# A new hand-written order for an attention and gated-MLP kernel, with idle products as words of the order

## The chip, the cores and the metric

One core of a Trainium2 chip runs the kernel. A core has five engines that run at the same time, each taking its own instructions in order: TensorE (PE, matrix products; its weight loads are listed as PEld), VectorE (DVE), ScalarE (ACT), GpSimd (POOL), and SyncE (SP), which here only starts DMA transfers. SBUF is the on-chip memory of 128 partitions; PSUM has eight banks per partition into which PE writes. The metric is the device time of one execution in microseconds, as the median of several runs.

## The reference

Attention with normalised q and k, and then a gated MLP whose second half is mixed along the sequence. Cut to what matters:

```python
# q, k, v: (8, 12, 448, 64)
q_n, k_n = rmsnorm(q, g_q), rmsnorm(k, g_k)
scores = (1 / sqrt(64)) * q_n @ k_n.transpose(0, 1, 3, 2)
attn = softmax(scores)
x = (attn @ v).transpose(0, 2, 1, 3).reshape(8, 448, 768)

h = maximum(x @ w_in, 0)                  # 768 -> 1024
u, v2 = h[..., :512], h[..., 512:]
v_n = (v2 - mean(v2)) / sqrt(var(v2) + 1e-6)
v_s = einsum('ts,bsd->btd', w_spatial, v_n) + b_spatial[None, :, None]
out = (u * v_s) @ w_out                   # 512 -> 768
```

rmsnorm divides a row of 64 by its root mean square and multiplies by a vector of gains.

## The kernel before

The work is cut into 24 groups, three for each of the eight batch entries; a group holds four heads. In a group, q and k are loaded (word L, 448 KB each), squared (Q, on ACT, DVE or POOL), summed over each row of 64 (R, DVE), turned into 1/rms by a logarithm and an exponential (I and J, ACT), and multiplied by it (N, DVE or POOL). Then they are transposed, either on PE (P, followed by the eviction K on DVE) or by a DMA transpose (T; Z then applies the gains to k). A group has seven score words: S.G.u on PE makes two PSUM banks of scores from 8 products of 64 rows by 32 columns, and E.G.u takes the exponential of both banks on ACT. Three kinds of passes on PE sum over the exponentials of one such unit: s with ones (the softmax's denominators), a and b with the two halves of v, which F converts to bf16. D and d on ACT invert the denominators through a logarithm and an exponential, X on DVE multiplies and leaves the MLP's input. Groups 0 and 1 pass one group at a time; from group 2 on, two groups share a pass.

The MLP of a batch entry b is made of V (the half v2, 2 products a word), c (its relu), B (statistics), M and m (1/std), A (normalising); U (the half u, 2 products a word) and u (its relu); H (the mixing along the sequence, 4 products), G (the gate, DVE), O (the output product, 4 products), o (eviction) and t (store). W.b holds the last 64 rows of the products V of entry b and O of entry b - 1.

Small letters l, q, r, i, j, n, p, k are the same steps for group 0, cut into two halves (r = 0 and 1) so that work can begin on the first half of the load. z.n and h.n are idle products: n products of the identity into a PSUM bank (448 and 64 columns, lines 250 to 259), whose result nobody reads.

All of this is issued from one string, PLAN, a list of words. A word is name.arguments/slots/engine: `E.3.6/3/a` is the exponential of unit 6 of group 3 into buffer 3 on ACT (a is ACT, v DVE, g POOL, s SP). The loop at lines 719 to 722 issues word by word, so that the order of the words of one engine in the string is the order in which that engine runs them:

```python
for word in PLAN.split():
    name, sl, e = (word.split("/") + ["", ""])[:3]
    name, *args = name.split(".")
    here["op_" + name]([int(x, 36) for x in sl], e, *map(int, args))
```

Waits between engines follow from the tiles that the words read and write, and from one more rule: the elementwise passes of DVE and POOL over SBUF (Q, N, F, Z, A) each wait for the last such pass of the other engine in the string (`port`, lines 281 to 285). The numbers of buffers are fixed (`SLOTS`, line 152): 10 raw loads, 22 buffers of exponentials, 8 PSUM banks shared by all.

Lines to follow the text by: 253 idle products, 293 loads of a group, 306 half loads of group 0, 365 and 367 copies (on ACT, on another engine), 384 and 386 squares, 397 and 403 sums, 410 and 415 logarithm and exponential of I and J, 430 and 438 normalising passes, 449 and 457 transposes on PE, 468 evictions of k, 510 scores, 518 exponentials, 545 summing passes, 564 and 568 D and d, 574 X, 581 relu on ACT, 590 V, 619 W, 656 U, 670 H, 684 O.

Of the kernel before, what the change touches and what calls it, by code (L numbers as in the profile page):

```python
# [22 lines left out]
l.0.0/0/a l.1.0/1 gl.0//g l.0.1//a l.1.1 L.1.0/2 gl.1//g setup L.1.1/3 L.2.1/4 L.2.0/5 z.12/0 L.3.0/6 q.0.0/0/v  # L23
L.3.1/7 q.1.0/1/a r.0.0 L.4.0/8 r.1.0 q.0.1//a L.4.1/9 i.0//a r.0.1 j.0//a q.1.1//v n.0.0//v r.1.1 p.0.0/0 Q.1.0/2/a
n.1.0//g gA gB/1 i.1//a R.1.0 p.1.0/2 j.1//a k.0.0/0/a n.0.1//g gC Q.1.1/0/a k.1.0/0/v n.1.1//g L.0.2/0 p.0.1/0
Q.2.1/1/a R.1.1 S.0.1/12 L.5.0/1 p.1.1/3 E.0.1/0/a Q.2.0/2/g k.0.1//v I.1//a k.1.1//v J.1//a R.2.1 Q.3.0/0/a
S.0.3/01 S.0.2/23 N.1.0/0/g S.0.4/45 S.0.5/67 E.0.3/1/a R.2.0 E.0.4/2/a S.0.0/01 ws N.1.1/1/v L.1.2/2 E.0.5/3/a
P.1.0/4 wi.0.3 R.3.0 I.2//a L.6.0/3 P.1.1/5 Q.3.1/1/g E.0.0/4/a S.0.6/67 J.2//a K.1.1/1/v E.0.2/5/a s.0.0.0/0 s.0.3.0
 K.1.0/1/v N.2.1/2/g E.0.6/6/a s.0.5.0 R.3.1 S.1.6/12 s.0.1.0 s.0.4.0 E.1.6/7/a S.1.1/34 S.1.2/56 s.0.6.0 wi.1.3
s.0.2.0 N.2.0/3/v L.5.1/4 I.3//a S.1.0/12 D.0/0/a P.2.1/7 J.3//a E.1.2/8/a P.2.0/0 Q.4.0/2/g K.2.1/2/v E.1.1/9/a  # L30
S.1.3/56 K.2.0/2/v Y.3/7 E.1.3/a/a wi.1.0 N.3.0/0/v S.2.6/34 E.1.0/b/a Y.0/0 N.3.1/1/v T.3.0/3 E.2.6/c/a Y.2/1 F.0//v
d.0//a L.7.1/5 y.3//v S.2.0/23 Q.5.0/0/g R.4.0 S.1.5/45 wb/1 E.2.0/d/a Y.1/6 L.6.1/6 y.2//v L.7.0/7 E.1.5/e/a L.2.2/0
Q.6.0/1/g S.1.4/12 y.1//v b.0.2.0/3 y.0//v E.1.4/f/a P.3.1/7 R.5.0 Q.4.1/2/a a.0.4.0/0 a.0.2.0 S.2.2/12 K.3.1/3/v
Q.5.1/0/g b.0.1.0 b.0.6.0 E.2.2/g/a b.0.3.0 R.4.1 S.2.3/45 s.1.6.0/6 a.0.0.0 E.2.3/h/a a.0.1.0 a.0.6.0 R.6.0 a.0.5.0
# [718 lines left out]
```

## Time and profile before

| | |
|---|---|
| median of 3 runs | 271.17 us (270.94 to 273.24) |
| the profiled execution | 269.62 us, its span 267.8 us |
| busy PE / DVE / ACT / POOL | 252.0 / 210.1 / 219.4 / 123.9 us |
| weight loads on PE | 127.0 us |
| mean granted clock of PE | 0.977 |
| moved by DMA | 55.93 MB, 209 GB/s on average |

A profile is one execution. The span goes from the first to the last instruction; the execution's own time has 1.8 us more around it. A row of a timeline is: start, length, engine, line of the kernel, operation, output<-input, shapes, count, and in brackets the idle time of that engine ahead of it with what ended it. A row of the groups is: line, engine, operation, names, shapes, count, then busy microseconds and the mean nanoseconds of one, then the idle time ahead of such instructions and what ended most of it. In the chain of waits a row is start, length and what. A product's busy time is modelled with its pipeline, so products that follow each other closely are told by the distance of their starts.

### The profile page before, as it was taken

To read this page: it belongs to the slowest core of one execution; us is meant where nothing else is said; L and a number is where in the kernel's file an instruction comes from. 1 tells how busy PE (TensorE), PEld (TensorE's weight loads), DVE (VectorE), ACT (ScalarE), POOL (GpSimd) and SP (SyncE) were. 2 spreads that over 40 slices of the span, in tenths; PEclk is the share of its full clock that TensorE was granted. 3 is DMA by queue.
4 is the path that set the end of the run, shared out by engine and by line. 5 is a ranking of instruction groups with operands and counts; after the bars stand their busy time and mean duration, and the time that the engine had idled before them with its cause. 6 is when DMAs were issued, how large, how long until landed. Compare 5 with 4: busy or idle time off the path is not lost.

```text
span 267.8 us, 9983 instructions
## 1 busy us (share of the span) xinstructions
PE 252.0 (94%) x4282; PEld 127.0 (47%) x4282; DVE 210.1 (78%) x367; ACT 219.4 (82%) x362; POOL 123.9 (46%) x96
## 2 busy tenths in 40 slices
PE   5598998999999997999999999999999999999993
PEld 2355454345444553445544554445445645555551
DVE  5998988899999996997998777999567463636861
ACT  4889899799999997898999899999899989521512
POOL 2795975668775587644734765443450000000000
PEclk9959799999999999999999999999999999999998
DMA  7999999999999999999999989999661041120135
GB/s 258 385 319 236 299 227 222 279 200 239 229 271 197 291 243 253 242 283 277 282 221 254 267 197 231 316 236 167 228 126 68 4 179 32 62 117 2 54 154 206
DMA packets 60446, 55.93 MB, mean 209 GB/s; under 512 B 36465, under 2 KB 56242, under 8 KB 60402
## 3 DMA queue, kind: packets, MB, share of 16 engines
q1 hardware_dynamic: 58082, 51.98, 77.0%
q0 software_dynamic: 1952, 2.76, 6.1%
q8 instruction: 33, 0.54, 0.9%
q10 hardware_dynamic: 368, 0.56, 0.6%
q14 instruction: 11, 0.09, 0.1%
HBM read 38.55 MB, written 11.01 MB: 185 GB/s over the span
## 4 chain that ended last, share of the span: by engine, by line
PE 86%; ACT 5%; DVE 4%; issue 2%; DMA 2%; DVEq 0%
PE ps L545 17%; PE ps L510 14%; PE ps L656 14%; PE ps L684 12%; PE ps L590 12%; PE ps L670 9%; PE ps L619 5%; ACT et L518 4%; DMA raw<-in_q_dram 2%; PE ps L449 1%; DVE ss L397 1%; DVE nrm L430 1%; DVE kT L468 1%; DVE ss L403 0%; DVE qT L367 0%
## 5 line engine op out<-in xcount | busy, mean ns | idle before, releaser
L518 ACT ACTIVATE et<-ps 128x896 bf16<-128x896 f32 x168 | 145.5, 919 | 11.1 <-PE ps L510 10.2
L430 POOL TENSOR_TENSOR nrm<-raw,rs 128x896 bf16<-128x896 f32 x31 | 52.1, 1688 | 39.1 <-DVE nrm L430 13.7
L510 PE MATMUL ps<-qT,kT 64*32 64x448 bf16 x1344 | 60.5, 365 | 4.4 <-DVE kT L468 1.6
L386 POOL TENSOR_TENSOR sqt<-raw 128x896 f32<-128x896 f32 x29 | 48.4, 1678 | 18.2 <-DVE nrm L430 5.2
L397 DVE TENSOR_REDUCE ss<-sqt 128x14 f32<-128x896 f32 x46 | 48.7, 1074 | 0.0
L545 PE MATMUL ps<-et,vt 64*32 64x448 bf16 x1344 | 47.2, 352 | 0.4 <-issue 0.4
L656 PE MATMUL ps<-xt,w_in 128*128 128x448 bf16 x192 | 42.7, 353 | 0.0
L590 PE MATMUL ps<-w_in,xt 128*128 128x512 bf16 x144 | 37.5, 380 | 0.6 <-issue 0.6
L684 PE MATMUL ps<-w_out,gt 128*128 128x384 bf16 x192 | 36.6, 327 | 0.2 <-issue 0.2
L574 DVE TENSOR_TENSOR xt<-ps,rc 128x448 bf16<-128x448 f32 x48 | 27.9, 616 | 8.8 <-ACT rc L568 4.5
L510 PEld LDWEIGHTS <-kT 64*32 64x32 bf16 x1344 | 20.4, 91 | 29.1 <-issue 19.9
L545 PEld LDWEIGHTS <-vt 64*32 64x32 bf16 x1344 | 21.0, 93 | 14.7 <-issue 3.3
L670 PE MATMUL ps<-w_spT,vn 128*128 128x448 bf16 (+1 forms) x128 | 27.3, 353 | 0.0
L656 PEld LDWEIGHTS <-w_in 128*128 128x128 bf16 x192 | 17.6, 98 | 19.9 <-issue 4.9
L545 PE MATMUL ps<-et,ones 64*32 64x448 bf16 x672 | 25.9, 356 | 0.5 <-ACT et L518 0.5
L367 DVE COPY os<-ps 128x384 f32<-128x384 f32 (+2 forms) x36 | 19.6, 548 | 8.3 <-PE ps L619 2.9
L684 PEld LDWEIGHTS <-gt 128*128 128x128 bf16 x192 | 17.8, 98 | 16.8 <-issue 4.7
L675 DVE TENSOR_TENSOR gt<-ps,us 128x448 bf16<-128x448 f32 x32 | 19.0, 618 | 8.2 <-PE ps L670 7.3
L631 DVE BATCH_NORM_STATS2 s<-vs 128x6 f32<-128x512 bf16 (+1 forms) x32 | 21.8, 680 | 3.4 <-ACT vs L581 3.0
L365 ACT ACTIVATE os<-ps 128x384 f32<-128x384 f32 (+2 forms) x29 | 13.9, 485 | 10.2 <-PE ps L684 7.2
L590 PEld LDWEIGHTS <-xt 128*128 128x128 bf16 x144 | 12.6, 98 | 18.1 <-issue 6.7
L581 ACT ACTIVATE vs<-ps 128x512 bf16<-128x512 f32 (+1 forms) x20 | 11.8, 596 | 9.1 <-PE ps L590 8.7
(64 smaller groups left out, 260.0 us busy)
## 6 DMA issues: line engine op xcount, KB each, us to landing
raw<-in_q_dram SPq DMA_DIRECT2D x23, 448.0 KB, 6.4
raw<-in_k_dram SPq DMA_DIRECT2D x23, 448.0 KB, 6.2
out_dram<-os SPq DMA_DIRECT2D x23, 384.0 KB, 3.4
raw<-in_v_dram SPq DMA_DIRECT2D x13, 448.0 KB, 6.1
raw<-in_v_dram SPq DMA_DIRECT2D x22, 224.0 KB, 5.2
out_dram<-os SPq DMA_DIRECT2D x9, 192.0 KB, 2.7
w_in<-in_moe_w_in_dram POOLq DMA_DIRECT2D x8, 192.0 KB, 5.8
w_out<-in_moe_w_out_dram POOLq DMA_DIRECT2D x1, 768.0 KB, 12.8
```

What stands on the lines that cost most here:

```text
L386: port(eng, eng.tensor_tensor(out=t, in0=x, in1=x, op=ALU.mult))
L397: dve.tensor_reduce(out=sss[G % 3][:, i].rearrange("p r c -> p (r c)"), in_=sqt[where.pop(("sq", G, i))].rearrange("p r (c d) -> p (r c) d ...
L430: port(eng, eng.tensor_tensor(out=nrm[sl[0]].rearrange("p c r d -> p r c d"), in0=raw[where["raw", G, i]].rearrange("p r (c d) -> p r c d" ...
L510: pe.matmul(out=ps[at:at + 32, sl[n], 0:S], lhsT=kT[64 * r:64 * r + 64, c, 64 * hh + 32 * x:64 * hh + 32 * x + 32], rhs=qT[64 * r:64 * r + ...
L518: act.activation(out=ets[sl[0]].rearrange("q r (p c) -> q r p c", c=C), in_=ps[:, a:b + 1:b - a, 0:S].rearrange("q r (c p) -> q r p c", c= ...
L545: pe.matmul(out=ps[32 * l:32 * l + 32, where[kind, G][0], 0:S], lhsT=w, rhs=et_of(G, r, c)[at:at + 64], start=(n == 1), stop=(n == C), til ...
L574: dve.tensor_tensor(out=xts[b % 2][:, 2 * g + half, :], in0=ps[:, where.pop(("ab"[half], G))[0], 0:S], in1=rcs[where["rc", G]], op=ALU.mult)
L590: pe.matmul(out=ps[:, bank, :], lhsT=xts[b % 2][:, j, 128 * m:128 * m + 128], rhs=w_in[:, j % 2, j // 2, DH:], start=(n == 1 and j == 2 * ...
L631: dve.bn_stats(out=s6, in_=vss[b % SLOTS["vs"]][rows, m, :])
L656: pe.matmul(out=ps[:, bank, 0:S], lhsT=w_in[:, j % 2, j // 2, 128 * f:128 * f + 128], rhs=xts[b % 2][:, j, :], start=(n == 1 and j == 2 * ...
L670: pe.matmul(out=ps[:, sl[0], 0:S], lhsT=vns[b % SLOTS["vn"]][rows, m, 128 * f:128 * f + 128], rhs=w_spT[rows, m, :], start=(m == 0), stop= ...
L684: pe.matmul(out=ps[:, sl[0], 0:384], lhsT=gts[b % 2][:, f, 128 * m:128 * m + 128], rhs=w_out[:, f, 384 * h:384 * h + 384], start=(f == 0), ...
```

## The change

The string PLAN is replaced as a whole; the functions, `SECOND`, `SLOTS` and the sizes stay. The same words stand in both plans (1,640 and 1,644) except for the idle products: one word of 12 (z.12) before; z.11 and h.6 in its place, and z.4, z.3 and z.1 later. Each engine's order is new, and so is the choice of engine for some words: squares Q on ACT, DVE, POOL go from 12, 5, 29 to 9, 8, 29; normalising passes N on DVE, POOL from 15, 31 to 14, 32; conversions of v (F) on ACT, DVE, POOL from 1, 8, 15 to 1, 4, 19; relus of v2 (c) on ACT, DVE from 20, 12 to 17, 15; relus of u from 14, 18 to 12, 20; two of the 17 Z go from DVE to ACT. In group 0 three of the four half squares are on ACT and one on POOL (two and two on ACT and DVE before); all four half normalising passes are on POOL and all four copies k on DVE.

The lines of the plan that hold the beginning and the words which the prediction speaks of (the rest is rewritten in the same manner):

```diff
@@ -20,132 +20,132 @@
-l.0.0/0/a l.1.0/1 gl.0//g l.0.1//a l.1.1 L.1.0/2 gl.1//g setup L.1.1/3 L.2.1/4 L.2.0/5 z.12/0 L.3.0/6 q.0.0/0/v
-L.3.1/7 q.1.0/1/a r.0.0 L.4.0/8 r.1.0 q.0.1//a L.4.1/9 i.0//a r.0.1 j.0//a q.1.1//v n.0.0//v r.1.1 p.0.0/0 Q.1.0/2/a
-n.1.0//g gA gB/1 i.1//a R.1.0 p.1.0/2 j.1//a k.0.0/0/a n.0.1//g gC Q.1.1/0/a k.1.0/0/v n.1.1//g L.0.2/0 p.0.1/0
-Q.2.1/1/a R.1.1 S.0.1/12 L.5.0/1 p.1.1/3 E.0.1/0/a Q.2.0/2/g k.0.1//v I.1//a k.1.1//v J.1//a R.2.1 Q.3.0/0/a
-S.0.3/01 S.0.2/23 N.1.0/0/g S.0.4/45 S.0.5/67 E.0.3/1/a R.2.0 E.0.4/2/a S.0.0/01 ws N.1.1/1/v L.1.2/2 E.0.5/3/a
...
-L.8.0/0 E.3.6/3/a Q.7.0/0/g K.4.0/0/v b.1.6.0 s.2.0.1 s.2.2.1 X.1.0 s.2.5.1 I.6//a S.3.1/56 J.5//a s.2.3.1 X.1.1
-s.2.6.1 E.3.1/f/a S.4.1/12 F.3//g R.7.1 E.4.1/4/a s.2.1.1 S.4.4/56 b.2.6.1/07 N.5.1/1/v b.2.0.1 E.4.4/1/a
...
-J.7//a V.0.0.0/4 E.4.5/8/a N.7.1/2/v L.9.1/4 V.0.2.0 d.3//a V.0.1.0/5 L.10.1/1 X.2.1 V.0.0.1 N.6.0/3/g L.5.2/5 R.8.1
-V.0.1.1 Q.8.0/2/a V.0.0.2 S.4.6/01 X.3.1 c.0.0//a W.0/2 T.6.0/2 Z.5/1/v E.4.6/a/a X.3.0 N.6.1/1/g R.8.0 L.4.2/3
-c.0.3//a S.5.6/01 S.5.3/67 E.5.6/9/a V.0.2.2 wo L.11.0/6 P.7.1/2 c.0.2//v E.5.3/e/a Q.9.0/0/g B.0.3 S.4.0/01 S.5.2/34
...
-u.0.3//a A.0.2 S.5.0/12 I.8//a S.5.1/34 A.0.3 S.5.4/67 E.5.0/3/a A.0.0 U.0.0.2 A.0.1 U.0.1.0 E.5.4/h/a R.9.1 U.0.1.1
-P.6.1/1 E.5.1/j/a u.0.0//v F.4//g H.0.2/2 Q.10.1/1/a N.7.0/0/g H.0.0/3 L.11.1/3 G.0.2 J.8//a F.5//a K.6.1/3/v
...
+l.0.0/0/a l.1.0/1 gl.0//g l.0.1//a wb/0 l.1.1 gl.1//g setup L.1.0/2 L.1.1/3 L.2.1/4 z.11/0 h.6 L.2.0/5 q.0.0/0/a
+L.1.2/6 q.1.0/1/a r.0.0 L.3.0/7 r.1.0 L.3.1/8 q.0.1//g L.6.0/9 i.0//a j.0//a q.1.1//a r.0.1 n.0.0//g gA r.1.1 n.1.0//g
+gB/0 p.0.0/1 Q.1.0/2/a gC p.1.0/0 i.1//a R.1.0 j.1//a Q.1.1/0/a n.0.1//g z.4/2 k.0.0/0/v Q.2.1/1/a n.1.1//g L.5.0/0
+p.0.1/2 k.1.0/0/v R.1.1 ws S.0.1/01 L.4.0/1 p.1.1/3 E.0.1/0/a Q.2.0/2/g k.0.1//v S.0.2/45 I.1//a z.3/6 k.1.1//v J.1//a
...
+s.0.0.0 R.3.0 S.1.3/23 N.2.1/2/g E.0.4/6/a S.1.6/45 s.0.5.0 z.1/7 R.3.1 E.1.6/7/a S.1.1/01 s.0.3.0 s.0.6.0 s.0.2.0
...
+d.1//a S.3.1/34 N.5.1/0/g b.1.4.0 s.2.4.1 E.3.1/5/a S.3.6/01 X.1.1 s.2.3.1 X.1.0 E.3.6/c/a S.4.4/23 s.2.1.1 R.6.1
...
+I.6//a V.0.2.1 J.7//a X.3.1 N.7.0/3/g a.2.4.1 S.4.5/56 a.2.2.1 E.4.5/9/a V.0.1.1/2 X.2.0 V.0.1.0 X.3.0 Q.8.1/2/a
+V.0.1.2 N.7.1/2/g L.10.1/8 R.8.0 V.0.0.2 J.6//a c.0.1//a S.4.6/34 S.5.3/56 R.8.1 E.4.6/1/a W.0/7 L.9.0/5 E.5.3/4/a
+N.6.0/0/v S.5.6/23 c.0.3//a P.7.1/4 c.0.0//v L.13.1/9 E.5.6/b/a Q.9.1/0/g V.0.2.2 T.6.0/2 K.7.1/2/v S.5.2/56 c.0.2//a
...
+u.0.0//a Q.9.0/1/g S.5.4/34 S.5.1/56 u.0.2//v H.0.0/2 E.5.1/f/a u.0.3//v H.0.2/1 E.5.4/c/a N.8.0/2/g S.6.4/56 G.0.2
```

230 lines of the change are left out of this document (116 added, 114 removed).

## The prediction, made before the changed kernel had run

> **What bounds the kernel now.** I read the page's slices first (they show where the granted clock falls), then the busy times of these stretches, then the timelines of ScalarE (ACT) and TensorE (PE) where PE idles.
>
> ```profile
> core 0 of [0], span 267.8 us
> core 0: us, PE busy (x) PEld busy (x) DVE busy (x) ACT busy (x) POOL busy (x), PEclk, DMA share, GB/s
> 6.48:13.31 6.83, 3.88 (x44) 2.29 (x43) 6.62 (x12) 5.76 (x11) 4.71 (x5) 1.00 1.06 385
> 13.31:20.14 6.83, 6.83 (x98) 3.60 (x102) 6.25 (x8) 5.99 (x10) 6.45 (x6) 0.50 1.12 319
> 20.14:26.96 6.82, 5.57 (x131) 3.46 (x116) 5.98 (x9) 6.58 (x11) 3.57 (x4) 1.00 1.17 232
> 26.96:30.38 3.42, 3.06 (x44) 1.48 (x47) 3.10 (x7) 2.81 (x4) 3.42 (x3) 0.50 0.83 253
> 37.20:44.03 6.83, 5.66 (x170) 3.32 (x170) 6.03 (x10) 6.68 (x12) 4.03 (x4) 1.00 1.04 267
> 44.00:54.00 10.00, 9.32 (x177) 4.23 (x154) 7.98 (x12) 8.27 (x15) 6.56 (x5) 1.00 1.02 233
> 80.00:240.00 160.00, 158.14 (x2924) 79.08 (x2923) 124.55 (x225) 141.09 (x233) 68.00 (x47) 1.00 0.84 200
> 240.00:263.40 23.40, 23.40 (x138) 12.21 (x136) 14.98 (x31) 7.47 (x16) 0.00 (x0) 1.00 0.24 85
> ```
>
> PEld is the weight loads, DVE is VectorE, POOL GpSimd. There are two regimes. From 44 us to 263.4 us PE is busy all but a few microseconds, so each microsecond by which that regime starts earlier is worth a microsecond, and its length is a count of products that the change keeps. Before 44 us PE has holes and ACT does not: 5.99 of 6.83, 6.58 of 6.82, 6.68 of 6.83. In this part PE also runs at half clock twice, from 13.31 to 20.14 and from 26.96 to 30.38. The change's idle products aim at that.
>
> ```profile
> 14.30 2.54 ACT L518 ACTIVATE et<-ps 128x896 bf16<-128x896 f32 x3 [0.53 <-PE ps L510]
> ...
> 19.88 0.92 ACT L518 ACTIVATE et<-ps 128x896 bf16<-128x896 f32 x1 [0.31 <-PE ps L510]
> ...
> 21.22 0.54 ACT L564 ACTIVATE rc<-ps 128x448 f32<-128x448 f32 x1 [0.22 <-PE ps L545]
> ...
> 30.49 1.73 ACT L518 ACTIVATE et<-ps 128x896 bf16<-128x896 f32 x2 [0.73 <-PE ps L510]
> ```
>
> ```profile
> 42.32 0.37 PE L545 MATMUL ps<-et,ones 64*32 64x448 bf16 x4 [0.51 <-ACT et L518]
> ```
>
> The last exponential of groups 2 and 3 (E.3.1) ends shortly before 42.32 us, and PE has waited 0.51 us for it. This is where the ACT regime hands over to the PE regime. What ACT has to do up to there, plus its idle time up to there (0.53 + 0.31 + 0.22 + 0.73 = 1.79 us, all behind PE), sets the start of a PE regime of fixed length.
>
> **The change, part by part.** The plan is a list of words, each engine taking its own in order, so I compare what stands ahead of the same point in both plans.
>
> ```profile
> L581 ACT ACTIVATE vs<-ps 128x512 bf16<-128x512 f32 x14 | 8.4, 600 | 8.8 <-PE ps L590 8.7
> L581 ACT ACTIVATE us<-ps 128x448 bf16<-128x448 f32 x14 | 7.4, 548 | 5.6 <-PE ps L656 5.6
> L410 ACT ACTIVATE ls<-ss,eps 128x28 f32<-128x28 f32 x23 | 7.3, 324 | 0.2 <-DVE ss L397 0.2
> L415 ACT ACTIVATE rs<-ls 128x28 f32<-128x28 f32 x23 | 5.1, 228 | 0.3
> ...
> L384 ACT ACTIVATE sqt<-raw 128x448 f32<-128x448 f32 x2 | 1.2, 577 | 3.0 <-DMA raw<-in_k_dram 1.8 <-DMA raw<-in_q_dram 1.1
> ...
> L365 ACT ACTIVATE qT<-ps 64x896 bf16<-64x896 bf16 x1 | 0.9, 892 | 0.0
> ```
>
> *ACT's list up to the handover.* Both plans have 28 exponentials up to the last of groups 2 and 3 (E.3.1 before, E.3.6 after). The new list has one more half square (+0.577), no copy of qT (-0.892, now k.0.0 on DVE) and one logarithm fewer (-0.324): -0.64 us. Behind this point PE has the same work in both plans but for two summing passes, 0.4 us.
>
> *Idle products.* Their prices come from the first word and from ordinary products of the same 448 columns.
>
> ```profile
> 4.63 0.15 PEld L253 LDWEIGHTS <-ident 128*128 128x128 bf16 x1 [0.22 <-issue]
> 5.00 0.15 PEld L253 LDWEIGHTS <-ident 128*128 128x128 bf16 x1 [0.22 <-issue]
> ```
>
> ```profile
> 79.90 1.14 PE ps L656 x6
> 81.03 0.69 PE ps L510 x24
> 81.72 1.24 PE ps L656 x6
> ```
>
> The loads in the first word are 0.37 us apart, and 1.14 / 6 = 0.19 us is a product later on: half rate and full rate. The first word had 12 long products and gets 11, with 6 of 64 columns, a seventh as long: 11.9 in place of 12, no change. The eight later ones cost 8 x 0.19 = 1.5 us at full and 3.0 us at half rate. Seven of them (z.4, z.3) fall between 6.48 and 13.31 us, where PE idles 6.83 - 3.88 = 2.95 us, which hides 7 x 0.19 = 1.33 us; without that cover they would delay the scores behind them by 1.3 to 2.6 us. The eighth follows a summing pass of group 0: at most 0.4 us, in the ACT regime, taken as nothing.
>
> What they buy is the clock. With z.4, z.3 (1.33) and one score word moved up from behind 13.31 us (S.0.2, two sets of four at 0.19, 0.38), PE is busy 3.88 + 1.71 = 5.59 of 6.83 us, 82%. The rows stand on both sides of that: 5.57 of 6.82 was followed by half clock, 5.66 of 6.83 was not. So it is little better than even that the first half-clock stretch goes. If it goes, I count ACT's idle 0.53 (a second score word now stands ready ahead of S.0.3), 0.31 and 0.22 as gone, 1.06 us; not the 0.73, since nothing idle is added near 26.96. Bounds are 0 and 1.79 us.
>
> ```profile
> 13.30 2.91 PE L510 MATMUL ps<-qT,kT 64*32 64x448 bf16 x40 [1.30 <-DVE kT L468]
> ```
>
> The row shows PE's longest wait just before the drop, 1.30 us. The Trainium skill, TensorE: Matmul & The Clock Gate, Part 1: The HAM clock gate, says the clock halves after an idle window of about 3.4 us and returns after a busy one; by it, gaps as short as these cost no clock, and the idle products bring nothing. The trace disagrees with it here: the clock fell after a 1.30 us wait, and stayed at half through 6.83 us in which PE was busy throughout. By that rule the sum would be that of the second rival below.
>
> *The first score word.* DVE's list ahead of it loses two half squares and a half normalising pass and gains the copy k.0.0 (no row of its own here; by these two, about 0.62); POOL gains a half square and that normalising pass.
>
> ```profile
> 6.70 0.62 DVE L386 TENSOR_TENSOR sqt<-raw 128x448 f32<-128x448 f32 x1
> 7.23 0.62 DVE L438 TENSOR_TENSOR nrm<-raw,rs 128x448 bf16<-128x448 f32 x1
> ```
>
> ```profile
> L438 POOL TENSOR_TENSOR nrm<-raw,rs 128x448 bf16<-128x448 f32 x3 | 2.8, 937 | 5.0 <-DVE nrm L438 4.8 <-ACT rs L423 0.2
> ```
>
> If DVE alone set the start it would come 3 x 0.62 - 0.62 = 1.24 us earlier; if the normalising pass on POOL does, 0.94 - 0.62 = 0.32 us later. I take zero, since PE now has 4 x 0.19 = 0.76 us of idle products ahead of the transpose and the first score word. Both ends stay in the range. SP issues one small load (wb) ahead of the second half of k, and the group loads come in another order; with the DMA share at 1.06 they move the same bytes, and ACT, which now squares that half, has other work until then: nothing.
>
> *Later.* PE's switches between full products and the 64-row kinds cost: six products right after scores take 1.24 us, six after full products 1.14, so about 0.10 a switch. The plans have 92 and 95 of them: +0.3 us. ACT's list up to the last exponential of groups 4 and 5 (E.5.1, now E.5.4) grows: + 0.577 - 0.892 + 0.228 + 0.600 + 0.548 = +1.06 us.
>
> ```profile
> 59.26 2.54 ACT L518 ACTIVATE et<-ps 128x896 bf16<-128x896 f32 x3
> ```
>
> ```profile
> 62.69 0.95 PE L545 MATMUL ps<-et,ones 64*32 64x448 bf16 x32
> ```
>
> It ended at 61.80 us; its first use, the third pass of the lower row, is at 62.69 + 2 x 0.19 = 63.07 us: 1.27 us to spare. In the new kernel ACT is +1.06 - 1.06, PE 1.4 earlier: 0.1 us of wait, which I add.
>
> **The sum.** -0.64 - 1.06 + 0.3 + 0.1 = -1.3 us. The profiled execution took 269.62 us (span 267.8 and 1.8 around it) and would take 268.3. The timed runs' median, 271.17, is 1.55 us above it; nothing in the trace says why, so I carry the same difference over: 269.9 us. The case's own range is 267.8 (idle gain 1.79, start 1.24 earlier: -3.3) to 271.2 (no idle gain, start 0.32 later: +0.1).
>
> **Rivals.** *Slower: GpSimd's two normalising passes end last.* N.7.1 moves from DVE to POOL, directly behind N.7.0, and PE's transpose P.7.1 waits for it in line, with V.0.2.2 and scores of group 5 queued behind, for which ACT waits.
>
> ```profile
> 50.79 1.69 POOL L430 TENSOR_TENSOR nrm<-raw,rs 128x896 bf16<-128x896 f32 x1 [0.67 <-DVE kT L468]
> ```
>
> ```profile
> 52.55 0.60 PE L590 MATMUL ps<-w_in,xt 128*128 128x512 bf16 x2
> 52.99 0.55 PE L449 MATMUL ps<-ident,nrm 128*128 128x128 bf16 x7
> ```
>
> The new plan puts P.7.1 ahead of V.0.2.2, so PE gets there near 52.55 - 1.3 = 51.25 us. If POOL begins the pair as late as it began a pass before, 50.79 us, it ends at 50.79 + 2 x 1.69 = 54.17 us, PE waits 2.9 us, and the balance is +1.6: 272.8 us, or 274.5 with one more pass ahead of them. It decides from a start later than 51.25 - 3.38 = 47.87 us. For it: the pass in that row had to wait 0.67 us for DVE, and passes of the two engines are ordered against each other by the plan. Against it: the pair stands well ahead of its use.
>
> *The clock is as before.* The half-clock stretch stays, by the edge above or because the first word does not win the full clock in some execution. Then -0.64 + 0.3: 270.9 us. The same page, under What's actually happening, has the window free-running; whether it starts elsewhere in another execution no single trace shows.
>
> *Faster: PE's later holes close too.* They are 0.51 at 42.32, 10 - 9.32 = 0.68, and 160 - 158.14 = 1.86, 3.05 us in all. The new plan moves three relus of v and two of u from ACT to DVE (3 x 0.600 + 2 x 0.548 = 2.9 us), so ACT could be earlier at each. Half of it gives 268.4, all 266.8; I take 267.6. Against it: another order makes holes of its own, and from 240 to 263.40 us none is left to close.
>
> **Chances and range.** Forecast 0.40, clock as before 0.18, faster 0.17, slower 0.25. A measurement of this kernel tells about 1%, 2.7 us, from no change. Below 268.46 lie nearly all of the faster case (0.15) and a sixth of the forecast's (0.07); above 273.88 rather more than half of the slower case (0.14, where a further pass comes in); the rest is within. The range 267.2 to 273.8 leaves out a third of the faster case (0.06) and that part of the slower one (0.14).
>
> **What would show it.** Right: the granted clock stays 1.00 from 13.3 to 20 us, ACT's first wait behind L510 is gone, and PE's wait at the end of groups 2 and 3 comes 1.4 us sooner. Clock as before: 0.50 again in that stretch. Slower: a transpose at L449 with an idle time of 1 to 3 us near 51 us, released by GpSimd's L430. Faster: PE busy over 159 us of 80 to 240. The prediction is wrong at its root if PE is not busy throughout from 54 us on, or if the first exponential starts over a microsecond from its old place.

## The result, and the profile after

| | before | changed kernel |
|---|---|---|
| median | 271.06 us (269.57 to 273.24, 4 runs) | 284.42 us (281.48 to 287.91, 4 runs) |
| ratio, 95% interval | | 1.045 (1.033 to 1.057) |
| the profiled execution, span | 269.62, 267.8 us | 287.91, 286.1 us |
| busy PE / DVE / ACT / POOL | 252.0 / 210.1 / 219.4 / 123.9 us | 257.7 / 212.1 / 216.9 / 132.1 us |

The changed kernel is 4.5% slower; the forecast was 269.9 us, and the range ended at 273.8. A second profile (run after_again, below) is of 287.77 us with a span of 286.0 and has the same shape; both profiles are of executions some 3.4 us over the median, so the losses below may be smaller in a median execution.

The busy times by stretch of the changed kernel, with the columns of the prediction's first fence (one row more, 54 to 80 us):

```profile
6.48:13.31 6.83, 6.46 (x70) 3.55 (x76) 5.87 (x11) 5.69 (x11) 6.27 (x7) 1.00 1.04 387
13.31:20.14 6.83, 5.71 (x115) 2.65 (x99) 6.68 (x8) 6.61 (x12) 5.49 (x4) 1.00 1.12 321
20.14:26.96 6.82, 5.29 (x120) 3.47 (x113) 6.35 (x11) 6.82 (x11) 3.76 (x4) 1.00 1.00 273
26.96:30.38 3.42, 3.00 (x76) 1.58 (x77) 3.21 (x5) 3.42 (x6) 3.42 (x5) 1.00 1.12 249
44.00:54.00 10.00, 9.45 (x123) 3.54 (x107) 9.17 (x15) 8.75 (x16) 7.28 (x5) 1.00 1.00 269
54.00:80.00 26.00, 15.83 (x270) 7.33 (x276) 12.16 (x23) 13.00 (x24) 13.62 (x10) 0.80 1.20 203
80.00:240.00 160.00, 154.42 (x2823) 75.19 (x2808) 126.47 (x220) 142.06 (x228) 78.86 (x54) 1.00 0.86 198
```

and the row of before that the prediction did not show:

```profile
54.00:80.00 26.00, 26.00 (x431) 12.19 (x431) 24.22 (x42) 24.96 (x42) 19.32 (x13) 1.00 1.17 238
```

Up to 30 us PE keeps the full clock, and from 13.31 us on ACT is busier than before, as forecast. Then PE is busy for only 15.83 of the 26 us after 54 us, at a mean clock of 0.80, where it had been busy throughout, and for 154.42 of 160 us from 80 on, where it had 158.14. These are two separate losses, both in the stage of which the prediction had said that its length is a count of products.

The first loss, in the chain of waits of the changed kernel (start, length, what):

```profile
51.95 0.19 PE ps L449 x2
52.15 19.67 DMA qT<-nrm
71.82 0.04 issue
71.86 0.57 PE ps L510 x7
```

and in its timeline of PE, where S.6.4 waits for the transposed q of group 6:

```profile
61.50 0.92 PE L670 MATMUL ps<-w_spT,vn 128*128 128x448 bf16 x4 [0.50 <-DVE us L583]
71.86 0.57 PE L510 MATMUL ps<-qT,kT 64*32 64x448 bf16 x8 [9.45 <-DMA qT<-nrm]
```

The DMA transpose T.6.0 took 19.67 us from issue to landing, PE stood still for 9.45 us, and the clock was at half until 75.95 us. The timelines of SP and POOL show what was under way with it:

```profile
52.15 11.53 SPq L485 DMA_TRANSPOSE qT<-nrm  x2
```

```profile
53.36 0.83 POOL L334 DMA_DIRECT2D w_out<-in_moe_w_out_dram  x1
```

The first of the two transposes is T.6.0, the second T.7.0. T.6.0 and w_out's load (768 KB) were issued 1.2 us apart. SP was held for 11.53 us in issuing the two transposes; the issue of T.7.0 began at 57.73 us, close to the first packets of T.6.0 (57.75) and of the load (58.28). Before, the neighbours were these, on SP and on POOL:

```profile
51.30 1.26 SPq L485 DMA_TRANSPOSE qT<-nrm  x1
...
64.05 1.23 SPq L485 DMA_TRANSPOSE qT<-nrm  x1
```

```profile
52.42 0.83 POOL L334 DMA_DIRECT2D w_out<-in_moe_w_out_dram  x1
```

One transpose stood beside the load; the next was issued 13 us later.

To compare runs I use the time at equal work: every product of the plan but the idle ones is counted at full rate, and the table has the time at which a run starts the product after so much work, minus the same time in the profile of before. Work 8 is reached there at 21.0 us, 24 at 40.6, 40 at 59.2, 75 at 94.4, 140 at 162.1 and 220 at 242.6 us.

| work | changed | after_again | a_wo_late | a_then_b | mix_late |
|---|---|---|---|---|---|
| 8 | -0.60 | +0.99 | -0.49 | +0.06 | +0.27 |
| 24 | -1.30 | +0.60 | -0.12 | -0.14 | +0.75 |
| 40 | -1.41 | -0.85 | +0.30 | +0.23 | +1.13 |
| 50 | +10.88 | +12.22 | +0.47 | +0.53 | +1.12 |
| 75 | +11.03 | +12.77 | +1.44 | +0.98 | +1.14 |
| 140 | +12.97 | +12.88 | +2.35 | +4.55 | +6.04 |
| 220 | +17.80 | +17.70 | +7.17 | +4.50 | +11.39 |

The last two columns are two mixes of the orders (below). In the changed kernel's profile the lead at work 40 is 1.41 us, which is what the prediction had ("PE 1.4 earlier"); 12.3 us are lost between work 40 and 50, and 4.8 us between 140 and 220.

### The profile page after: what moved, and what is told of

Its sections match the earlier page's. It is cut to its first block, busy times and chain, and to the rows that moved or that the text cites. A ratio compares the mean times of both kernels' runs of the same rounds, so it can differ in the third digit from the quotient of the medians.

```text
span 286.1 us, 9991 instructions
## 1 busy us (share of the span) xinstructions
PE 257.7 (90%) x4295; PEld 128.4 (45%) x4295; DVE 212.1 (74%) x366; ACT 216.9 (76%) x355; POOL 132.1 (46%) x104
## 4 chain that ended last, share of the span: by engine, by line
PE 75%; DMA 14%; ACT 4%; DVE 2%; issue 2%; POOL 1%; SPq 0%; DVEq 0%
PE ps L545 17%; PE ps L510 12%; PE ps L656 12%; PE ps L684 11%; PE ps L590 9%; DMA qT<-nrm 9%; PE ps L670 8%; PE ps L619 4%; DMA gt<-in_moe_w_spatial_dram 4%; ACT et L518 3%; DMA raw<-in_q_dram 2%; POOL nrm L438 1%; ACT os L365 0%; DVE nrm L430 0%; DVE kT L468 0%
## 5 line engine op out<-in xcount | busy, mean ns | idle before, releaser
L510 PE MATMUL ps<-qT,kT 64*32 64x448 bf16 x1344 | 62.0, 356 | 15.3 <-DMA qT<-nrm 9.9
L386 POOL TENSOR_TENSOR sqt<-raw 128x896 f32<-128x896 f32 (+1 forms) x30 | 49.5, 1654 | 43.4 <-DVE kT L468 18.5
L430 POOL TENSOR_TENSOR nrm<-raw,rs 128x896 bf16<-128x896 f32 x32 | 53.6, 1687 | 24.3 <-ACT rs L415 19.5
L397 DVE TENSOR_REDUCE ss<-sqt 128x14 f32<-128x896 f32 x46 | 48.6, 1073 | 10.2 <-ACT sqt L384 10.2
L545 PE MATMUL ps<-et,vt 64*32 64x448 bf16 x1344 | 46.4, 349 | 2.7 <-issue 2.3
L656 PE MATMUL ps<-xt,w_in 128*128 128x448 bf16 x192 | 43.3, 353 | 0.0
L510 PEld LDWEIGHTS <-kT 64*32 64x32 bf16 x1344 | 21.9, 90 | 47.5 <-issue 29.8
L574 DVE TENSOR_TENSOR xt<-ps,rc 128x448 bf16<-128x448 f32 x48 | 28.2, 618 | 13.5 <-PE ps L545 7.5
L545 PEld LDWEIGHTS <-vt 64*32 64x32 bf16 x1344 | 22.4, 92 | 16.0 <-issue 5.2
L656 PEld LDWEIGHTS <-w_in 128*128 128x128 bf16 x192 | 17.6, 98 | 18.7 <-issue 4.2
L321 POOL CAST vt<-raw 128x896 bf16<-128x896 f32 x19 | 17.7, 929 | 17.6 <-DVE nrm L430 8.5
L583 DVE TENSOR_SCALAR us<-ps 128x448 bf16<-128x448 f32 x20 | 11.9, 613 | 11.8 <-PE ps L656 11.2
```

Of the source, the lines that this page charges most:

```text
L386: port(eng, eng.tensor_tensor(out=t, in0=x, in1=x, op=ALU.mult))
L397: dve.tensor_reduce(out=sss[G % 3][:, i].rearrange("p r c -> p (r c)"), in_=sqt[where.pop(("sq", G, i))].rearrange("p r (c d) -> p (r c) d ...
L430: port(eng, eng.tensor_tensor(out=nrm[sl[0]].rearrange("p c r d -> p r c d"), in0=raw[where["raw", G, i]].rearrange("p r (c d) -> p r c d" ...
L510: pe.matmul(out=ps[at:at + 32, sl[n], 0:S], lhsT=kT[64 * r:64 * r + 64, c, 64 * hh + 32 * x:64 * hh + 32 * x + 32], rhs=qT[64 * r:64 * r + ...
L545: pe.matmul(out=ps[32 * l:32 * l + 32, where[kind, G][0], 0:S], lhsT=w, rhs=et_of(G, r, c)[at:at + 64], start=(n == 1), stop=(n == C), til ...
L574: dve.tensor_tensor(out=xts[b % 2][:, 2 * g + half, :], in0=ps[:, where.pop(("ab"[half], G))[0], 0:S], in1=rcs[where["rc", G]], op=ALU.mult)
```

## Experiments

Theory A: the transposes and w_out's load spoil each other when they are under way together. Theory B: the transposes are late because of the plain loads ahead of them in SP's queue. Ratios are against runs of before on the same chip. Words left out of a diff are unchanged, and a word that moves takes its instructions with it on its own engine only.

**Which DMA makes T.6.0 late.**

a_wo_early:

```diff
-U.0.1.0/7 wo T.7.0/3
+U.0.1.0/7 T.7.0/3
...
-R.1.1 ws S.0.1/01
+R.1.1 ws wo S.0.1/01
```

> The changed kernel with one word moved: w_out's load (wo) is issued directly behind ws, near 20 us, in place of 53 us, so that it is not under way when T.6.0 and T.7.0 are. Theory A (the two transposes and w_out's load spoil each other when they overlap): T.6.0 lands in 5 to 8 us in place of 19.7, the wait of 9.45 us in front of S.6.4 is under 1 us, and the time falls by 9 to 13 us to about 272 to 275, less what the earlier load takes from the loads of the first 40 us (up to 3 us). Theory B (the transposes are late because eight plain loads stand ahead of them in the queue): T.6.0 still takes 12 us or more, the wait stays above 5 us, and the time stays above 279.

280.98 us, 1.042 (1.031 to 1.054). T.6.0 lands in 10.5 us in place of 19.7 and the wait ahead of S.6.4 is 0.3 us, which lies between the theories for the landing and is theory A's for the wait. The time is theory B's, but for another reason: the early load holds up the words of the first 30 us: PE waits 3.7 us for w_spT, and the run is 4.8 us behind at work 40. Taking w_out's load away nearly halved the landing. What went is the stretch behind the first packet: T.6.0's first packet comes 5.9 us after its issue here and 5.6 us in the changed kernel, with the same eight plain loads ahead of it, but from there the two transposes take 4.8 us to their last packet in place of 14.7.

a_T_first:

```diff
-L.10.1/8
+T.7.0/3
...
-L.13.1/9
...
-T.6.0/2 K.7.1/2/v
+T.6.0/2 L.10.1/8 L.13.1/9 K.7.1/2/v
...
-wo T.7.0/3 U.0.3.1/0
+wo U.0.3.1/0
```

> The changed kernel with SP's order changed alone: T.7.0 and T.6.0 are issued ahead of the loads L.10.1 and L.13.1 (T.7.0, L.9.0, T.6.0, L.10.1, L.13.1), some 3 us sooner, wo as it is. Theory A: both transposes are done, or nearly, before w_out's packets flow near 58 us; the wait in front of S.6.4 is under 2 us and the time is 270 to 275. Theory B: the same or a part of it, since two loads fewer stand ahead, of about 1.3 us each: the landing gets shorter by 3 us only, the wait is 6 us, the time about 279. Theory C (the loss is in the order of the compute engines): the time stays above 280.

280.93 us, 1.038 (1.028 to 1.047). No wait for qT is left, as theory A had it, yet the time misses its 270 to 275 and is what theory C named: the two loads that were put back now come late, ACT waits 2.68 us for k's and PE 1.96 us for ACT at 69.24 us, and the loss behind work 140 (below) is untouched.

a_wo_late:

```diff
-U.0.1.0/7 wo T.7.0/3
+U.0.1.0/7 T.7.0/3
...
-F.5//g J.8//a
+F.5//g wo J.8//a
```

> The changed kernel with w_out's load issued some 5 us later, behind GpSimd's copy of v for group 5 (F.5), near 59 us; nothing ahead of the two transposes is altered. Theory A (overlap): T.6.0 lands in 8 to 11 us, the wait in front of S.6.4 is under 1.5 us, and the time is 272 to 277. Theory B (the loads ahead): landing above 14 us, a wait above 5 us, the time above 279.

276.22 us, 1.018 (1.008 to 1.029), as theory A had it: 8.2 us off the changed kernel by one word, and nothing ahead of the transposes altered. In its table of the transposes and its timeline of PE:

```profile
DMA to landing us min/median/max: 2.9/4.9/8.7
```

```profile
63.40 0.38 PE L510 MATMUL ps<-qT,kT 64*32 64x448 bf16 x8
...
71.15 0.82 PE L684 MATMUL ps<-w_out,gt 128*128 128x384 bf16 x4 [0.90 <-DMA w_out<-in_moe_w_out_dram]
```

S.6.4 starts at 63.40 without a wait; the later load costs 0.90 us at its own first use.

after_again is the changed kernel itself.

> The changed kernel itself, measured beside the others: 281 to 288 us, with T.6.0 landing in over 12 us and a wait of 3 to 10 us in front of S.6.4. If it comes out at 276 or less, the stall is not a property of the order but of single executions.

284.44 us, 1.042 (1.030 to 1.055); T.6.0 lands in 20.8 us and the wait is 11.09 us, a little over the 10 expected. The stall belongs to the order.

**What the overlap is.** Three runs move only wo in the kernel before; one moves it a little in the changed one.

```diff
 b_wo_late
-V.0.2.2 wo L.11.0/6
+V.0.2.2 L.11.0/6
...
+Q.9.1/1/g wo
```

> The kernel before with one word moved: w_out's load (wo) is issued about 3 us later, behind Q.9.1, so that its packets flow while T.7.0 and T.8.1 (issued at 64 and 66 us) are under way. Theory A: these two take over 10 us to land or to issue in place of some 5, the load itself gets longer, and the kernel is 3 us or more slower than before (274 or above). Theory B: the queue ahead of them is unchanged, so their landing is as before, within 2 us, and the time is within 1.5 us of before.

270.5 us, 1.003 (0.994 to 1.012). It told nothing: w_out's packets ran from 60.36 to 65.27 us, and T.7.0's began at 65.24.

```diff
 b_wo_later
-V.0.2.2 wo L.11.0/6
+V.0.2.2 L.11.0/6
...
+F.4//g wo
```

> The kernel before with w_out's load issued behind GpSimd's copy of v for group 4 (F.4), near 61.5 us, so that its packets flow from about 65.5 us, together with those of T.7.0 and T.8.1 (issued at 64 and 65.7 us). Theory A (overlap costs): the packets of both get slower, one of the transposes takes over 9 us to land or to issue, w_out takes over 9 us from its first packet, and the kernel is 4 us or more slower than before. Theory B (only what stands ahead in the queue counts): transposes land in 7 us or less, w_out comes some 1 to 2 us late for O.0.0.1, and the kernel is at most 2 us slower.

275.12 us, 1.024 (1.015 to 1.034). Slower as theory A had it, but not in its way: w_out's packets began first (64.06 to 68.73 us), T.7.0's waited until 67.65, and no transpose took over 8.3 us. Its profile is 1.5 us behind before at work 75 and 4.2 us at 140, so most of it is lost far behind the transposes, in several waits of 0.6 to 1.6 us.

a_wo_bit and b_wo_mid turn the order of the two beginnings round:

```diff
 a_wo_bit
-E.5.6/b/a Q.9.1/0/g
+E.5.6/b/a wo Q.9.1/0/g
 b_wo_mid
-N.7.0/0/g
+N.7.0/0/g wo
```

> The changed kernel with w_out's load issued only some 1.7 us earlier, ahead of Q.9.1 on GpSimd (51.7 in place of 53.4 us), so that its packets flow from about 56.6 us, before those of T.6.0 (57.5). Theory E (interleaving: a transpose that is under way when the other queue's load begins is stretched, and stretches it): now the load runs first, in 5 to 7 us, T.6.0 lands in 9 to 12 us, the wait in front of S.6.4 is 0 to 3 us, and the time 275 to 279. Theory F (bytes ahead of the transpose alone): more bytes stand ahead of T.6.0 than before, so it lands no earlier, the wait stays above 7 us, the time above 281.

> The kernel before with w_out's load issued behind N.7.0 on GpSimd, near 63.3 us, so that its packets flow from about 66 us, when T.7.0's (from 64.3) are under way and T.8.1's follow. Theory E: both are stretched as in the changed kernel: w_out takes over 9 us from its first packet to its last, a transpose lands in over 9 us, and the kernel is 5 us or more slower than before. Theory F: w_out in 5 to 6 us, transposes in at most 8 us, and a loss of 2 to 5 us, since w_out comes late for O.0.0.1.

a_wo_bit: 280.78 us, 1.037 (1.027 to 1.046). T.6.0 lands in 12.4 us, a little over theory E's 12, and PE waits 2.86 us, within its bounds; the load takes 7.8 us in place of 5 to 7, and the time is 1.8 us above theory E's bound and 0.2 us short of theory F's. b_wo_mid: 275.76 us, 1.019 (1.007 to 1.031), slower by 5.6 us, as theory E had it. Its slowest transpose, in the table of the transposes, and its timeline of PE, where the late load itself is what PE waits for:

```profile
DMA to landing us min/median/max: 2.9/5.0/11.0
```

```profile
73.98 1.46 PE L684 MATMUL ps<-w_out,gt 128*128 128x384 bf16 x4 [4.54 <-DMA w_out<-in_moe_w_out_dram]
```

The packets, counted from the traces (w_out has 512 of 1,536 bytes; transposes have packets of 256 bytes, plain loads of SP's queue 1,792). The column "by the sum" is an estimate: all three kinds of packets that began during the load, at their usual times of 0.134, 0.018 and 0.074 us (the medians in before), on 16 engines.

| run | w_out, first to last packet | us | by the sum | 256-byte packets meanwhile, mean | which began first |
|---|---|---|---|---|---|
| a_wo_early | 18.65 to 29.11 us | 10.5 | 8.7 | none | |
| before | 57.72 to 64.91 | 7.2 | 7.0 | none | |
| b_wo_late | 60.36 to 65.27 | 4.9 | 5.4 | 19, 0.018 us | load |
| b_wo_later | 64.06 to 68.73 | 4.7 | 5.0 | 511, 0.022 | load |
| a_wo_bit | 56.83 to 64.65 | 7.8 | 8.0 | 292, 0.018 | load |
| a_no_later_z (below) | 58.34 to 64.64 | 6.3 | 6.0 | 803, 0.035 | load |
| mix_52 (below) | 58.68 to 65.11 | 6.4 | 6.7 | 473, 0.031 | transpose, by 0.38 us, 421 packets done |
| a_T_first | 59.63 to 68.19 | 8.6 | 7.5 | 381, 0.019 | transposes, 1,416 packets done |
| a_wo_late | 62.19 to 69.28 | 7.1 | 5.7 | 166, 0.062 | transposes, 1,718 packets done |
| b_wo_mid | 64.41 to 73.57 | 9.2 | 5.8 | 1,310, 0.060 | transpose, by 0.24 us |
| changed | 58.28 to 71.79 | 13.5 | 6.1 | 1,302, 0.120 | transpose, by 0.53 us |
| after_again | 58.36 to 73.27 | 14.9 | 5.5 | 949, 0.117 | transpose, by 0.95 us |

T.6.0 and T.7.0 together have 1,792 packets, and so have T.7.0 and T.8.1 in the runs b_. In the last three rows the load came in when the transposes had just begun, and both were stretched: the load took 3.4 to 9.4 us more than the sum, and the two transposes 10.2 to 16.5 us from first to last packet, where they take 3.0 to 5.3 in before, b_wo_late, b_wo_later, a_wo_bit, a_wo_late, a_no_later_z and a_wo_early. In the other rows the load lies within 1.8 us of the sum. (A packet's mean time says less: the median of the 256-byte packets is 0.018 us, but 896 of them in a row with none of w_out's among them have means from 0.018 to 0.097 us in the 19 profiles, and take 0.8 to 5.2 us.) So the overlap of the two is what costs. That it matters which begins first fits most of these rows and is not proved by them: in mix_52 a transpose began first and the load kept to the sum.

**The loss behind 140.** Mixes of the two orders: words of one plan up to a point, then the rest in the other's order, with buffers and banks renamed where the two plans clash, and a few words at the joint put behind what they need.

mix_late is the old order's first 677 words and then the new order; a_then_b is the new order's first 677 words, with wo as in a_wo_late, and then the old order.

> The old order up to 103 us (677 words), then the remaining words in the new order. If the changed kernel's losses behind 100 us (5.4 us of waits of TensorE for ScalarE and VectorE and for instructions between 167 and 246 us in its trace, the same to 0.01 us in the run with the transposes issued earlier, whose stall near 62 us is gone) belong to the new order itself, this is 4 to 7 us slower than before: 273.5 to 277. If they come of the lateness that the stall near 62 us leaves behind, it is within 1.5 us of before.

280.28 us, 1.033 (1.023 to 1.043). More than the 4 to 7 us expected: 5.4 us of it behind work 140, and most of the rest around 110 us, at the joint, where PE waits 2.96 us for DVE's X and 1.73 us for a kT.

> The changed kernel with w_out's load issued later, up to 115 us of its time (677 words), then the remaining words in the old order. If the 4.7 us behind 140 us belong to the new order there, this is 4 to 5.5 us faster than the 276.2 us of a_wo_late: 270.5 to 272.5. If they belong to what the first 677 words leave behind, within 1 us of 276.

273.37 us, 1.011 (1.006 to 1.015), 2.9 us under a_wo_late: less than expected, since between work 75 and 140 its profile loses 3.6 us (a wait of 1.53 us near 106 us, and half clock behind it). Behind 140 its loss is nil. The same piece of work, in the busy times by stretch of before, a_wo_late, mix_late and a_then_b:

```profile
162.10:222.60 60.50, 60.50 (x1098) 29.88 (x1088) 44.41 (x80) 56.75 (x91) 17.76 (x14) 1.00 0.69 166
```

```profile
164.50:229.80 65.30, 62.79 (x1141) 30.46 (x1126) 45.63 (x84) 56.03 (x85) 22.83 (x17) 1.00 0.63 150
```

```profile
168.20:234.00 65.80, 62.84 (x1127) 30.53 (x1112) 45.46 (x84) 55.99 (x85) 22.31 (x17) 1.00 0.67 147
```

```profile
166.70:227.10 60.40, 59.78 (x1093) 29.92 (x1098) 44.17 (x79) 56.68 (x91) 17.83 (x14) 1.00 0.76 165
```

and ACT's waits in these stretches, of before and of a_wo_late:

```profile
ACT et L518 <- PE ps L510: 2.3, 6, 0.6
```

```profile
ACT et L518 <- PE ps L510: 7.6, 16, 0.9
```

The new order needs 65.3 to 65.8 us for what the old one does in 60.4 to 60.5, whatever came ahead. ACT is no busier (56.0 against 56.7 us), but waits 16 times for scores in place of 6, and PE waits in turn for the banks that ACT and DVE have not yet read. PE's waits in this stretch of a_wo_late, of which before's has none:

```profile
PE ps L510 <- ACT et L518: 1.5, 3, 0.9
PE ps L510 <- DVE xt L574: 0.8, 1, 0.8
```

These rows leave out short waits, and busy times are modelled. Counted from the products' columns at full rate, PE's gaps in these stretches are 3.2 us in before and 4.6 in a_then_b, but 7.2 in a_wo_late and 7.7 in mix_late; 2.6 and 2.9 us of the last two end with an exponential, where before has 0.2, and 1.2 us in each with an X.

a_banks keeps the order of a_wo_late and gives each tile from S.10.2 on the bank that has been free longest (203 words):

```diff
-S.17.0/23
+S.17.0/01
...
-S.16.4/23
+S.16.4/25
```

> The changed kernel with w_out's load issued later (as in the run a_wo_late), and from S.10.2 on (about 106 us) every PSUM tile in the bank that has been free longest; the order of all words is the same, 203 words change their bank. Theory C (the late waits of TensorE are waits for a bank that the changed plan gives again too soon: S.17.0 waits for X.15.1 in bank 3 while banks 2, 4 and 7 have been free longer): the 4.7 us lost between 164 and 230 us fall below 1.5, and the time is 272 to 274 against 276.2. Theory D (the order itself holds ScalarE and TensorE up, whatever the bank): within 1 us of 276.

314.43 us, 1.163 (1.153 to 1.173), and it decides nothing between C and D. Of the score words that changed, 66 got two banks that do not lie side by side, and PE then waits for exponentials, also with products that read none:

```profile
PE ps L545 <- ACT et L518: 12.6, 17, 2.2
...
PE ps L656 <- ACT et L518: 5.4, 7, 1.6
```

U (L656) reads no exponential. In all seven of its waits the bank that U writes lies between the two that the exponential reads (U.2.2.0, for one, writes bank 4, and E.10.3 reads banks 0 and 5). So an exponential that reads two banks apart is ordered against what writes a bank between them. Whether another choice of side-by-side banks would help the changed plan was not tested, and which of its words cause the waits stays open.

**The early gain.** a_no_later_z leaves out idle products; b_idle adds some to the kernel before:

```diff
 a_no_later_z
-n.0.1//g z.4/2 k.0.0/0/v
+n.0.1//g k.0.0/0/v
...
-I.1//a z.3/6 k.1.1//v
+I.1//a k.1.1//v
...
-s.0.5.0 z.1/7 R.3.1
+s.0.5.0 R.3.1
 b_idle
+z.2/5 gB/1
...
+z.5/7 S.0.3/01
...
+z.1/7 S.1.3/56
...
+z.3/1 Y.2/1
...
+z.1/7 S.1.4/12
```

> The changed kernel without its eight later idle products (z.4/2, z.3/6, z.1/7). If they buy the clock as the prediction says, the granted clock is 0.50 again from about 13 to 20 us, and the work that the changed kernel has done by 57.8 us is done some 1 us later; if the new order alone keeps PE busy enough, the clock stays at 1.00 and that point is within 0.3 us. The large wait near 62 us is not touched: the time stays at 281 to 288 either way.

> The kernel before with twelve idle products added where its TensorE waits (2 ahead of gB, 5 ahead of S.0.3, 1 ahead of S.1.3, 3 ahead of Y.2, 1 ahead of S.1.4) and nothing else changed: the prediction's idle term by itself. If it holds, the granted clock is 1.00 from 13 to 30 us and the time 0.5 to 1.8 us below before, ratio 0.993 to 0.998. Rival: ScalarE's list sets the handover whatever the clock, ratio 1.000 within 0.002. Rival: the idle products stand in front of score words that are ready and cost more than they bring, ratio above 1.002.

a_no_later_z: 286.61 us (282.15 and 291.07), within the 281 to 288 expected. b_idle: 271.78 us, 1.001 (0.997 to 1.005), whose median is what the first rival named (ScalarE's list sets the handover whatever the clock), though the interval reaches into the other two cases. Their clocks by stretch, a_no_later_z first:

```profile
7.17:10.59 3.42, 2.10 (x29) 1.68 (x28) 2.94 (x6) 2.63 (x5) 2.62 (x4) 1.00 1.03 388
10.59:20.83 10.24, 10.14 (x126) 4.45 (x127) 8.90 (x11) 8.49 (x14) 8.49 (x7) 0.50 1.10 345
```

```profile
8.48:25.54 17.06, 11.77 (x187) 6.20 (x186) 15.67 (x20) 15.28 (x25) 13.22 (x13) 1.00 1.11 325
25.54:35.78 10.24, 10.24 (x136) 5.00 (x140) 6.18 (x10) 5.78 (x7) 6.22 (x6) 0.50 0.99 221
```

Without the idle products the clock is at half for 10.24 us, and with them in the old order it is full to 25.54 us: they do hold it. In time this shows little. a_no_later_z is 0.7 us ahead of before at work 40, against 1.41 and 0.85 with them. The profile of b_idle, of an execution of 274.38 us, was 0.97 us ahead at work 8, and then PE waited 3.2 us for w_spatial's load, which also cost the clock:

```profile
PE ps L352 <- DMA gt<-in_moe_w_spatial_dram: 3.2, 1, 3.2
```

That wait need not explain the median: the executions of mix_32, next, kept the clock (a median of 0.998 over the whole kernel against 0.978 of before beside them) and are no faster, though the joint of its two orders may hide a gain.

mix_32 and mix_52 keep the new order for 185 and 319 words, up to 32 and 52 us, and then go on in the old one.

> The new order up to 32 us (the first 185 words, with the idle products), and from there the remaining words in the old order; buffers and PSUM banks that the two orders give differently are renamed. If the prediction's terms up to the handover hold and its error lies wholly behind 58 us, this is 1.0 to 2.0 us faster than before (ratio 0.993 to 0.996), with the granted clock at 1.00 from 13 to 20 us. If the early part of the new order is worth nothing in most executions, the ratio is 1.000 within 0.004. If the joint between the two orders costs something, slower than 1.005.

> The new order up to 52 us (319 words), then the old one. It holds the new order's loads up to 52 us, which stand ahead of T.6.0, and the old distance between T.6.0, w_out and T.7.0. Theory A (the overlap of the transposes with w_out's load is what costs): T.6.0 lands in at most 10 us, no wait over 1.5 us in front of S.6.4, and the time is 268 to 271. Theory B (the loads ahead of the transposes cost): T.6.0 takes over 12 us, a wait of 3 us or more, and 273 or above.

mix_32: 271.79 us, 1.006 (1.002 to 1.010), which fits its third case; mix_52: 277.44 us, 1.023 (1.014 to 1.032). mix_32's profile, of an execution of 279.54 us, lay 3.0 us behind before at work 2 already; five of its score words got banks that lie apart. In mix_52 T.6.0 took 12.4 us, as theory B had it, and T.7.0 13.0, but PE did not wait 1.5 us for either; its wait of 2.72 us, ahead of H, was for DVE. T.7.0's input was ready early, and it was issued 2.8 us behind T.6.0 and not 13, so that the run did not keep the old distance. The time is that of theory B, the place is that of neither: the joint of two orders has waits of its own, so these two say little of the prediction.

Two last runs ask what holds the start up. In after_again's timeline of DVE the small load of g ends a wait:

```profile
7.91 0.88 DVE L371 SCALAR_TENSOR_TENSOR g_row<-g_row 1x128 f32<-1x128 f32 x1 [1.23 <-DMA g_row<-in_g_k_dram]
8.72 0.60 DVE L403 TENSOR_REDUCE ss<-sqt 128x7 f32<-128x448 f32 x1
```

The change put gA (L371) ahead of the last half reduction r.1.1 (L403), which now waits with it. In the eleven profiles with this start, the four in which gA waits under 0.3 us have the first exponential by 11.66 us, and the six in which it waits over 1.2 us have it at 12.13 or later. The two runs move gA; mix_32_gA also puts four of mix_32's five score words on adjacent banks, and four more words on other banks to make room.

```diff
 a_wo_gA (on a_wo_late) and mix_32_gA (on mix_32)
-n.0.0//g gA r.1.1 n.1.0//g
+n.0.0//g r.1.1 gA n.1.0//g
```

> The changed kernel with w_out's load later (as a_wo_late, 276.22 us) and one more word moved: VectorE's gA behind r.1.1. If the wait for the load of g is what delays the start, the first exponential begins by 11.8 us, VectorE's wait for g_row ahead of r.1.1 is gone, and the median is 0.5 to 1.5 us lower: 274.7 to 275.7. If something else delays the start in these executions, it stays at 276 to 277 and the first exponential is late in some profiles as before.

> The run mix_32 (new order to 32 us, then the old one; 1.0063 of before) with gA behind r.1.1, and four of the five score words whose renamed banks lay apart in adjacent banks again. If the start's wait is the cause, the first exponential begins by 11.8 us, and the prediction's early gain of 1 to 1.5 us shows: ratio 0.993 to 1.000. If the early gain is taken back on the way to the handover in any case (as in the runs a_then_b and b_idle), 1.001 to 1.005.

276.35 us, 1.016 (1.007 to 1.025), and 273.51 us, 1.007 (1.003 to 1.011). DVE's wait is gone in both profiles, but the first exponential starts at 12.22 and 12.14 us, not by 11.8, and neither is faster; 1.007 lies above both ranges that had been named. So gA's wait goes with the late starts and is not what the early gain is lost to. No version was found that beats the kernel before.

## Why the prediction was wrong

**The step that failed** is the sentence on the loads: "the group loads come in another order; with the DMA share at 1.06 they move the same bytes ... nothing". The bytes are the same; what they stand beside is not. T.6.0 and T.7.0 came to stand behind eight loads and beside w_out's load on the other queue: no term of the sum had this wait, and it measured 9.45 us, with half clock behind it. Moving w_out's load alone takes 8.2 of the 13.4 us back, and a_wo_early puts the part of the loads ahead at a landing of 10.5 us, which cost PE 0.3 us. Why the two stretch each other by more than the sum of their packets is open. That sentence was worked out for the first 13 us; the stretch at 52 us was never looked at, though the plan has wo and T.7.0 nine and ten words behind T.6.0.

**The frame failed too**: the PE regime's "length is a count of products that the change keeps". The same products took 4.8 us longer behind work 140 in the changed order, shown by mix_late and a_then_b from both sides. That PE waits for ACT and, less, for DVE to read a bank is seen in the rows; which words cause it is not known.

**The idle term, -1.06 us.** Half of the mechanism was right: the clock stayed at 1.00 where it had been 0.50, and fell back without the idle products. That this shortens the way to the handover did not show: by itself it measures 1.001 (0.997 to 1.005) of before, which leaves room for at most 0.8 us of gain. The step to the clock was luck in part. PE's busy time in 6.48 to 13.31 us was 6.46 us and not 5.59 (a score word had been counted at 0.38 us, where the row of 24 products, three words in 0.69 us, gives 0.23), and the edge at 82% is none: the changed kernel kept the full clock behind 5.29 of 6.82 us.

**ACT's list, -0.64 us, and the sum up to the handover.** In the changed kernel's profile the lead at work 40 was 1.41 us as forecast, in after_again 0.85. In the later variants of the changed kernel, whose words are the same up to 50 us but for single moves, it was +0.34 (a_T_first), +0.30 (a_wo_late), +1.00 (a_wo_bit) and +1.90 us (a_wo_gA). One profile had flattered it. The sign that PE's wait at the handover comes 1.4 us sooner can't be read: near there the changed kernel's PE waits only 0.24 us for an exponential, at 38.15. ACT's early waits for PE did shrink, from 0.53, 0.31, 0.22 and 0.73 us to one of 0.18 between 13 and 31 us.

**The start, taken as zero.** The old start has its first exponential at 11.32 to 11.79 us in six profiles; the new start at 11.24 to 14.67 in eleven. The bounds of -1.24 and +0.32 us left out the small load of g, since gA's move was not listed.

**The rivals.** The slower one had the right sign and the wrong place: GpSimd did N.7.0 and N.7.1 from 47.20 to 50.53 us, and P.7.1 at 51.89 had no wait. The clock as before did not occur in this profile. The faster one is out: PE is busy for 154.42 us, not over 159. The small terms of +0.3 for switches and +0.1 for groups 4 and 5 can't be told from the rest. The statement "wrong at its root if PE is not busy throughout from 54 us on" is what came true.

## What to carry to other kernels

When a plan is reordered, list for every DMA which transfers of other queues are under way with it, transposes above all, and not only how many bytes move: one load issued 6.1 us later was worth 8.2 us here. A stage in which one engine was always busy does not keep its length because its work is kept: here the same products took 4.8 us longer in another order, in which that engine and the one that empties its banks waited for each other. And a gain of 1 us read from one profile should be looked for in a second one before anything is built on it.

## What the runs showed of the hardware

A DMA transpose and a load of the other queue that have packets waiting at the same time take turns: in mix_52 from 60 to 62 us 223 packets of the load and 221 of the transpose began, in b_wo_mid from 66 to 68 us 200 and 198. The Trainium skill, DMA: Bandwidth & Descriptors, Queues, rings and completion order, says that a DMA engine takes turns between its queues, packet by packet; these counts fit that. By that the times of the two would add up. In nine of the table's twelve rows they do, within 1.8 us. In the three rows where the load began among the transposes' first packets they do not: 9.2 us for the load in place of 5.8, 13.5 in place of 6.1 and 14.9 in place of 5.5, and no run here shows why.

The granted clock falls after a stretch of 3.41 us in which PE streams for less than about 0.45 of the time. (The spells at half clock ahead of the kernel's end are 3.41, 6.83 or 10.24 us long, multiples of 3.41.) Worked out from the products' columns and the granted clock, so an estimate, 23 of the 25 falls in 19 profiles came after a share of at most 0.45 and the other two after 0.50 and 0.52, while only 9 of 1,413 stretches that kept the clock were that low. In before the share was 0.34 in the 3.41 us up to the fall at 13.31, with no wait of PE over 1.30 us in them: it needs no wait as long as the window.

PE's waits without a releaser end 2.2 to 3.3 us after a packet on the queue that loads code ("instruction" in the profile) has begun: so did all 42 such waits of over 0.6 us behind 14 us in 19 profiles, the longest of 2.8 us. In the changed kernel's timeline of PE:

```profile
111.89 1.12 PE L545 MATMUL ps<-et,vt 64*32 64x448 bf16 x34 [1.56 <-issue]
...
117.54 0.75 PE L510 MATMUL ps<-qT,kT 64*32 64x448 bf16 x22 [1.18 <-issue]
```

Code packets of 16 KB began 2.44 and 2.50 us ahead of these two. There are 33 such packets in the changed kernel, so this is hardly chance; that the engine waited for its code is what it suggests, and it was not tested.

An exponential of ScalarE that reads two PSUM banks apart holds up products that write a bank between them (seven waits of U in a_banks, 5.4 us). Whether the chip or the program's own ordering of its tiles does this, no run here shows.
